# Putting the state and output products of each attention chunk in one place between feed-forward matmuls (Trainium2, one core)

## The chip, the cores and the metric

The kernel runs on one core of one Trainium2 chip. The metric is the device time of one execution in microseconds (us), the median over runs of the same kernel. The core has five engines with queues of their own: TensorE (PE), VectorE (DVE), ScalarE (ACT), GpSimd (POOL) and SyncE (SP, which issues DMAs). An engine executes its instructions in program order; where it needs another engine's result it waits on a semaphore.

## The reference

```python
# B=4, H=8, S=768, D=48: 3072 tokens of 384
for t in range(S):
    cur = einsum('bhd,bhe->bhde', u[None] * k[:, :, t], v[:, :, t])
    y[:, :, t] = einsum('bhd,bhde->bhe', r[:, :, t], state + cur)
    state = w[None, :, :, None] * state + einsum('bhd,bhe->bhde', k[:, :, t], v[:, :, t])
x = y.transpose(0, 2, 1, 3).reshape(B * S, H * D)
x = square(maximum(x @ w_in, 0)) @ w_out          # 384 -> 2048 -> 384
logits = x @ w_gate
noisy = logits + log1p(exp(x @ w_noise)) * noise  # 8 experts
top2, top2_w = softmax over the two largest of noisy
for e in range(8):
    out[tokens of e] += top2_w * (maximum(x @ w1[e], 0) @ w2[e])
```

Three stages in a row: a linear attention with a decaying state, a dense feed-forward layer with a squared ReLU, and a mixture of eight experts of which each token uses two. All inputs and outputs are float32.

## The kernel before, in words

**Tiles.** The 3072 tokens are cut into 24 attention chunks q of 128 tokens (six to a sequence; c = q % 6 is the place in its sequence) and into 6 feed-forward blocks j of 512 tokens, four chunks each. A list written out by hand (HEAD) does chunks 0 to 3. Block j from 0 to 4 then computes its own feed-forward layer and, in between, chunks 4(j+1) to 4(j+1)+3 for the next block. The experts follow behind block 5.

**A feed-forward block.** For f from 0 to 15 the program writes: mm1, nine matmuls of w_in (L540) into a bank ph; gsplit, in which ACT takes the ReLU and the square (L545, L551, L553) and VectorE the low half of the square (L555); the pieces of slot 2f; mm2 of f − 2, nine matmuls of w_out (L571; for some f six matmuls of L565); the pieces of slot 2f + 1. All of attention, of the router and of the conversion of weights inside a block is such a piece.

**What sets the order.** CHUNKS (lines 36 to 47) is a table of numbers. Row 0 is for block 0, row 1 for block 1, row 2 for blocks 2 to 4. For each of the four chunks of a block it holds nine numbers, the times of the nine pieces pre, p_tr r, p_tr k, pre2, p_kv, p_a, p_y 0, p_y 1 and p_x: the whole part of a number is the slot, and the fraction is the order inside the slot. All engines follow this order, since a piece writes its instructions for all of them when its turn comes.

**The pieces that matter.** p_a are the scores of a chunk: eight matmuls (L459) into two banks, which VectorE copies through a mask into am (L463). p_kv is the state product: sixteen small matmuls (L503) into a bank; VectorE adds the old state Z (L510) and POOL multiplies by the decay (L511), or VectorE multiplies alone where c is 0 (L513); where c is 5 nothing is done. p_y 0 is the output product with the state: twelve matmuls of rT and Z (L477), none where c is 0. p_y 1 is the output product with the chunk itself: sixteen matmuls of am with v or vx (L477) into the bank that p_y 0 took, and it issues the load of v of chunk q + 2. p_x reads that bank (ACT L522, VectorE L523). p_tr transposes r or k: on TensorE into a bank for chunks under 8 (L439; the result is scaled by VectorE at L444, or copied by ACT at L448), else on VectorE (L430) with a scaling on POOL (L432).

**Banks.** p_kv, p_a, p_y, p_tr and the router take their PSUM banks from three with the tag att. Each takes the one whose turn it is, and waits until its former user has been read out.

**Beside it.** In block 0 the weights are split into a high and a low half: conv_w1 (ACT L272), conv_w2 (VectorE L279, L280, L281 and then L291 or L288) and conv_w3 (ACT L301, POOL L302), on weights that SP's queue loads ahead. In the blocks behind it the router of the block before runs: products with the gate weights (L604), small VectorE steps (L631 to L667), ranking products (L705 to L709) and indirect DMAs on POOL that send tokens to their experts (L731, L732).

Of the kernel before, what the change touches and what calls it, by code (L numbers as in the profile page):

```python
# [34 lines left out]

CHUNKS = (((0.72, 2.09, 0.63, 0.83, 1.23, 3.2, 1.96, 5.12, 6.53),
# [11 lines left out]

WHOLE = (1, 3, 5)
SPLIT_AT = (1.5, 5.5, 9.5)  # L50
# [42 lines left out]
def body(ctx, tc, r, k, v, w, u, w_in, w_out, w_gate, w_noise, noise, w1, w2, out):  # L93
# [961 lines left out]
    for j in range(NB):  # L1055
# [6 lines left out]
        if j + 1 < NB:  # L1062
            for i, at_ in enumerate(CHUNKS[min(j, 2)]):
                q = (j + 1) * TPB + i
# [194 lines left out]
```

## Time and profile before

| | |
|---|---|
| median of three runs | 958.3 us (957.74 to 958.36) |
| profiled execution | 953.54 us |
| its span | 951.7 us |
| granted TensorE clock, mean | 0.998 |
| PE busy | 938.6 us, 99% |
| PE weight loads | 806.6 us, 85% |
| DVE busy | 539.5 us, 57% |
| ACT busy | 433.6 us, 46% |
| POOL busy | 349.7 us, 37% |
| block 0 starts (first L540) | 32.94 us |
| blocks 1 to 5 start | 118.64, 202.76, 285.95, 368.72, 452.36 us |
| first matmul of the experts (L853) | 525.04 us |

The span is that of the traced instructions in one execution; the execution's own time is 1.8 us more. Times in the trace are us from the span's start. Busy time is the sum of an engine's instructions without overlap; matmuls are pipelined, so the 0.39 us that a single one shows is not what it costs in a row of them. The chain of waits gives starts and durations that follow each other.

### The profile page before, as it was taken

The numbers are of one execution on the slowest core, as the hardware profiler recorded it, in microseconds if no ns is written. First come the engines' busy times: TensorE is split into PE (matmuls) and PEld (weight loads), VectorE is DVE, ScalarE is ACT, GpSimd is POOL, SyncE is SP. The second block draws the span as 40 slices with busy tenths as digits, with TensorE's granted clock in tenths as the row PEclk, the third lists the DMA queues.
The fourth block names the chain that finished last, engine by engine and source line by source line (L and its number), as shares of the span: only waits on it lengthen the run. The fifth ranks groups of instructions, "written<-read, shape, count | busy, mean of one in ns | idle before, by whom it ended". The sixth has DMA issues, their size and how long they took to land.

```text
span 951.7 us, 17753 instructions
## 1 busy us (share of the span) xinstructions
PE 938.6 (99%) x6845; PEld 806.6 (85%) x6845; DVE 539.5 (57%) x982; ACT 433.6 (46%) x792; POOL 349.7 (37%) x406
## 2 busy tenths in 40 slices
PE   8899999999999999999999999999999999999996
PEld 7677787788878878887888899999999898989986
DVE  8999757646845663583344563554545455456420
ACT  5666655344434444343555642443434444344321
POOL 6665353554563454455030353122121221212112
PEclk9999999999999999999999999999999999999999
DMA  7655379942432463341035368466545555555112
GB/s 177 164 162 163 102 193 297 247 111 63 104 94 56 126 162 107 102 115 70 1 101 122 88 143 180 102 131 146 120 96 117 119 119 120 103 100 114 23 21 38
DMA packets 193234, 112.33 MB, mean 118 GB/s; under 512 B 131777, under 2 KB 185698, under 8 KB 193122
## 3 DMA queue, kind: packets, MB, share of 16 engines
q1 hardware_dynamic: 181698, 91.03, 38.1%
q0 software_dynamic: 10624, 19.74, 11.3%
q8 instruction: 75, 1.23, 0.6%
q14 instruction: 37, 0.30, 0.1%
q10 hardware_dynamic: 800, 0.02, 0.0%
HBM read 74.64 MB, written 36.12 MB: 116 GB/s over the span
## 4 chain that ended last, share of the span: by engine, by line
PE 92%; DVE 4%; DMA 1%; issue 1%; ACT 0%; POOL 0%; POOLq 0%; ACTq 0%; DVEq 0%; SPq 0%
PE ph L540 20%; PE ph L853 20%; PE xo L571 19%; PE y L910 14%; PE y L941 5%; PE att L477 3%; PE ph L941 2%; PE att L459 2%; PE y L853 2%; PE att L604 2%; PE xo L565 1%; PE att L954 1%; PE att L503 1%; DVE am L463 1%; DVE t L280 1%
## 5 line engine op out<-in xcount | busy, mean ns | idle before, releaser
L921 POOL DMA_INDIRECT out<-yt,id x56 | 87.2, 1556 | 298.9 <-ACT yt L919 255.3
L555 DVE TENSOR_TENSOR gl<-g,gh 128x512 fp32r<-128x512 f32 x90 | 76.5, 851 | 137.5 <-ACT gh L553 137.2
L896 DVE SCALAR_TENSOR_TENSOR hl<-ph,hh 128x512 fp32r<-128x512 f32 (+1 forms) x112 | 67.0, 599 | 114.7 <-ACT hh L895 114.5
L545 ACT ACTIVATE rt<-ph 128x512 f32<-128x512 f32 x96 | 57.2, 595 | 152.5 <-PE ph L540 152.4
L540 PE MATMUL ph<-x1h,wih 128*128 128x512 f32 x288 | 119.3, 414 | 0.0
L853 PE MATMUL ph<-xh,w0h 128*128 128x512 f32 (+1 forms) x336 | 118.9, 354 | 0.0
L853 PE MATMUL ph<-xh,w0l 128*128 128x512 f32 (+3 forms) x336 | 116.3, 346 | 0.0
L853 PE MATMUL ph<-xl,w0h 128*128 128x512 f32 (+3 forms) x336 | 116.2, 346 | 0.0
L540 PE MATMUL ph<-x1h,wil 128*128 128x512 f32 x288 | 112.4, 390 | 0.0
L540 PE MATMUL ph<-x1l,wih 128*128 128x512 f32 x288 | 112.3, 391 | 0.0
L571 PE MATMUL xo<-gh,wol 128*128 128x512 f32 x270 | 105.9, 392 | 0.0
L895 ACT ACTIVATE hh<-ph 128x512 fp32r<-128x512 f32 (+1 forms) x112 | 58.7, 525 | 90.1 <-PE ph L853 89.8
L910 PE MATMUL y<-w1h,hh 128*128 128x384 f32 x256 | 85.7, 335 | 0.0
L910 PE MATMUL y<-w1l,hh 128*128 128x384 f32 x256 | 85.6, 335 | 0.0
L910 PE MATMUL y<-w1h,hl 128*128 128x384 f32 x256 | 85.6, 334 | 0.0
L732 POOL DMA_INDIRECT sent<-row,si x48 | 50.1, 1044 | 61.4 <-DVE gl L555 45.0
L571 PE MATMUL xo<-gh,woh 128*128 128x512 f32 x180 | 71.5, 397 | 0.0
L571 PE MATMUL xo<-gl,woh 128*128 128x512 f32 x180 | 70.1, 390 | 0.0
L853 PEld LDWEIGHTS ph<-xh,w0l 128*128 128x128 f32 x336 | 63.2, 188 | 7.8
L853 PEld LDWEIGHTS ph<-xl,w0h 128*128 128x128 f32 x336 | 63.3, 188 | 7.4 <-DVE xl L830 0.7
L853 PEld LDWEIGHTS ph<-xh,w0h 128*128 128x128 f32 x336 | 63.2, 188 | 6.6
L540 PEld LDWEIGHTS ph<-x1h,wih 128*128 128x128 f32 x288 | 54.0, 188 | 16.4 <-issue 3.7
(234 smaller groups left out, 2144.2 us busy)
## 6 DMA issues: line engine op xcount, KB each, us to landing
ws<-in_moe_w SPq DMA_DIRECT2D x128, 96.0 KB, 2.7
ws<-in_moe_w SPq DMA_DIRECT2D x32, 384.0 KB, 5.6
sent<-zero SPq DMA_DIRECT2D x8, 1375.5 KB
G<-sent SPq DMA_DIRECT2D x36, 192.0 KB, 3.3
stg<-in_moe_w_in SPq DMA_DIRECT2D x8, 768.0 KB
stg<-in_moe_w_out SPq DMA_DIRECT2D x8, 768.0 KB, 4.4
out<-zero SPq DMA_DIRECT2D x5, 960.0 KB, 6.0
lv<-in_v SPq DMA_DIRECT2D x24, 192.0 KB, 2.8
```

The costliest lines, as they stand in the source:

```text
L477: nc.tensor.matmul(pb[32 * n:32 * n + 32, d, :], x, y, skip_group_check=True, **kw)
L540: nc.tensor.matmul(ph, wt[qi][:, d, sl], xt[j][:, d, :], start=(n == 0), stop=(n == 3 * KD - 1))
L545: nc.scalar.activation(rt, ph, AF.Relu)
L555: nc.vector.tensor_tensor(gl, g, gh.bitcast(F32), op=OP.subtract)
L571: nc.tensor.matmul(XO[j][:, d, :], wt[qi][:, fo, sl], gt, start=(f == 0 and n == 0), stop=(f == NF - 1 and n == 2))
L732: st = nc.gpsimd.indirect_dma_start(out=sent, in_=s["row"][:, i, :], in_offset=None, out_offset=bass.IndirectOffsetOnAxis(ap=s["si"][:, i, ...
L853: nc.tensor.matmul(ph[:, c], wt[:, d, sl], xt[:, d, c], start=(m == 0), stop=(m == 3 * KD - 1))
L895: nc.scalar.activation(hh[:, :n], ph, AF.Relu)
L896: nc.vector.scalar_tensor_tensor(hl[:, :n], ph, 0.0, hh[:, :n].bitcast(F32), op0=OP.max, op1=OP.subtract)
L910: nc.tensor.matmul(py, ht[:, sl], wt[:, fo, :], start=(m == 0), stop=(m == 3 * NF2 - 1))
L921: st = nc.gpsimd.indirect_dma_start(out=out, in_=yt, in_offset=None, compute_op=OP.add, out_offset=bass.IndirectOffsetOnAxis(ap=IDX[e, un] ...
L941: nc.tensor.matmul(py[d][:, c], wt[:, fo, sl], ht[:, c], start=(m == 0), stop=(m == 3 * NF2 - 1))
```

## The change

Only numbers of CHUNKS change. For each of the four chunks of a block, p_kv, p_y 0 and p_y 1 now follow each other in one slot, mostly the slot that p_y 1 had, and p_a stands in a slot of its own. Of the second chunk of block 1 that slot is 18 (p_y 1 was at 22.37), of the third 27 (29.33), and the third's scores go from 27.97 to 24.8. For the third chunk of blocks 2 to 4 the transposition of r goes from 11.43 to 13.6. TensorE has 7268 rows in the program before and after.

```diff
-CHUNKS = (((0.72, 2.09, 0.63, 0.83, 1.23, 3.2, 1.96, 5.12, 6.53),
-           (3.99, 6.52, 7.82, 8.89, 12.58, 10.32, 14.31, 14.42, 14.572),
-           (8.79, 15.58, 15.74, 17.5, 17.09, 19.34, 20.21, 22.27, 28.57),
+CHUNKS = (((0.72, 2.09, 0.63, 0.83, 5.1, 3.2, 5.11, 5.12, 6.53),
+           (3.99, 6.52, 7.82, 8.89, 14.3, 10.32, 14.31, 14.42, 14.572),
+           (8.79, 15.58, 15.74, 17.5, 22.25, 19.34, 22.26, 22.27, 28.57),
            (18.59, 17.86, 20.56, 22.96, 28.05, 24.63, 28.23, 28.43, 29.69)),
-          ((0.1, 3.42, 3.92, 4.42, 4.47, 7.61, 9.16, 10.56, 12.58),
-           (7.94, 9.19, 9.32, 12.56, 21.33, 13.02, 18.64, 22.37, 25.05),
-           (15.73, 15.29, 22.28, 20.4, 22.63, 27.97, 26.35, 29.33, 29.51),
-           (22.4, 22.61, 24.26, 25.89, 28.2, 28.47, 30.02, 30.16, 31.3)),
-          ((0.79, 1.41, 3.65, 3.78, 7.94, 5.73, 11.24, 13.52, 15.46),
-           (5.03, 9.3, 9.79, 10.52, 13.32, 11.71, 13.34, 15.87, 17.6),
-           (14.31, 11.43, 15.7, 15.49, 23.64, 21.16, 19.91, 25, 25.46),
-           (18.6, 17.96, 19.29, 23.4, 25.47, 26.59, 26.24, 29.22, 29.82)))
+          ((0.1, 3.42, 3.92, 4.42, 10.54, 7.61, 10.55, 10.56, 12.58),
+           (7.94, 9.19, 9.32, 12.56, 18.62, 13.02, 18.63, 18.64, 20.6),
+           (15.73, 15.29, 22.28, 20.4, 27.7, 24.8, 27.71, 27.72, 29.51),
+           (22.4, 22.61, 24.26, 25.89, 30.14, 28.47, 30.15, 30.16, 31.3)),
+          ((0.79, 1.41, 3.65, 3.78, 13.5, 5.73, 13.51, 13.52, 15.46),
+           (5.03, 9.3, 9.79, 10.52, 15.85, 11.71, 15.86, 15.87, 17.6),
+           (14.31, 13.6, 15.7, 15.49, 25.01, 21.16, 25.02, 25.03, 25.46),
+           (18.6, 17.96, 19.29, 23.4, 29.2, 26.59, 29.21, 29.22, 29.82)))
```

Three places of the order, as the programs of before and of the change have it. The first is VectorE in block 0, before: the two additions to the state of chunk 4 (Z from the bank att) stand behind a reduction for chunk 5 and ahead of a weight conversion (t is the weight being converted).

```order
L414 TENSOR_REDUCE dg<-ra 128x8
L510 TENSOR_TENSOR Z_202<-att,Z_201 48x4x48 x2
L279 TENSOR_SCALAR t_722<-t_722 128x768
L280 TENSOR_SCALAR t_722<-t_722 128x768
L281 SCALAR_TENSOR_TENSOR t_722<-stg,t_722 128x768
```

VectorE, block 0, after, fourteen rows further on:

```order
L288 SCALAR_TENSOR_TENSOR woh_141<-stg,t_774 128x768
L279 TENSOR_SCALAR t_802<-t_802 128x768
L280 TENSOR_SCALAR t_802<-t_802 128x768
L281 SCALAR_TENSOR_TENSOR t_802<-stg,t_802 128x768
L291 SCALAR_TENSOR_TENSOR t_802<-stg,t_802 128x768
L510 TENSOR_TENSOR Z_202<-att,Z_201 48x4x48 x2
L444 TENSOR_TENSOR rT<-att,pow 112x512
```

The additions moved behind three conversions of weights, a low half of the square (L555) and the copies of chunk 4's scores (L463).

The second place is TensorE in block 0, before: the transposition of chunk 5's keys (kp) between mm2 and mm1, with the queues on which its first row waits.

```order
L571 MATMUL xo<-gl,woh_140 128x512
L571 MATMUL xo<-gh,wol_148 128x512
L439 MATMUL att<-ident,kp_98 112x128 [waits PE_49,Pool_49]
L439 MATMUL att<-ident,kp_98 112x128 x3
L540 MATMUL ph<-x1h,wih_126 128x512 [waits Activation_49]
```

The same place after:

```order
L571 MATMUL xo<-gl,woh_140 128x512
L571 MATMUL xo<-gh,wol_148 128x512
L439 MATMUL att<-ident,kp_98 112x128 [waits DVE_49,PE_49,Pool_49]
L439 MATMUL att<-ident,kp_98 112x128 x3
L540 MATMUL ph<-x1h,wih_126 128x512 [waits Activation_49]
```

The rows around the transposition are the same, and its first row has a wait on VectorE more.

The third place is TensorE in block 1, as a piece of the difference: the scores of chunk 10 (att from rT and kT) and, in the same slots, what came there from elsewhere.

```order
 L540 MATMUL ph<-x1l,wih_130 128x512
 L540 MATMUL ph<-x1h,wil_138 128x512
+L459 MATMUL att<-rT,kT 128x128 x8
 L571 MATMUL xo<-gh,wol_153 128x512
 L571 MATMUL xo<-gl,wol_153 128x512
-L571 MATMUL xo<-gh,wor_1812 128x512
+L571 MATMUL xo<-gh,wor_1778 128x512
```

The scores stand there three nines ahead of their place before.

## Rows read from the trace of the kernel before

**Rows 1.** The page's part 4: shares of the span in the chain that ended last.

```profile
PE 92%; DVE 4%; DMA 1%; issue 1%; ACT 0%; POOL 0%; POOLq 0%; ACTq 0%; DVEq 0%; SPq 0%
```

**Rows 2.** Chain in order of time, block 4: start us, us, engine, tile, line, matmul records.

```profile
388.01 0.48 PE att L503 x32
388.49 2.28 PE ph L540 x9
...
398.46 0.79 PE att L477 x24
399.25 1.09 PE att L459 x16
400.34 2.27 PE ph L540 x9
...
404.65 0.48 PE att L503 x32
405.13 1.53 PE att L477 x56
406.66 2.27 PE ph L540 x9
408.93 2.04 PE xo L571 x9
410.97 1.01 PE att L477 x32
411.98 2.26 PE ph L540 x9
...
430.93 0.48 PE att L503 x32
431.41 2.26 PE ph L540 x9
```

**Rows 3.** The same chain in block 1.

```profile
173.39 0.48 PE att L503 x32
...
174.03 2.15 PE ph L540 x9
176.19 1.01 PE att L477 x32
177.20 0.34 PE att L503 x32
177.54 2.26 PE xo L571 x9
```

**Rows 4.** Timeline of VectorE, blocks 0 and 4: start us, us, instruction.

```profile
40.22 0.73 DVE L510 TENSOR_TENSOR Z<-att,Z 48x192 f32<-48x192 f32 x2
...
47.28 1.41 DVE L279 TENSOR_SCALAR t<-t 128x768 f32<-128x768 f32 x1
...
53.28 0.55 DVE L279 TENSOR_SCALAR t<-t 128x768 f32<-128x768 f32 x1
...
55.45 0.96 DVE L291 SCALAR_TENSOR_TENSOR t<-stg,t 128x768 int32<-128x768 int32 x1
...
410.66 0.19 DVE L656 SCALAR_TENSOR_TENSOR nl<-oh,nl 128x32 f32<-128x32 f32 x1
```

**Rows 5.** Timeline of TensorE, block 0.

```profile
53.21 0.60 PE L439 MATMUL att<-ident,kp 128*112 128x128 f32 x4
...
70.49 0.86 PE L477 MATMUL att<-rT,Z 112*32 112x128 f32 x24
...
73.02 0.50 PE L571 MATMUL xo<-gh,woh 128*128 128x512 f32 x1
```

**Rows 6.** Timeline of POOL, blocks 0, 1 and 4 (in brackets idle before, and what ended it).

```profile
50.93 1.62 POOL L396 TENSOR_TENSOR ra<-ra,ub 128x384 f32<-128x384 f32 x1
...
181.30 1.29 POOL L432 TENSOR_TENSOR kT<-kT,pow 112x512 f32<-112x512 f32 x1
...
405.63 1.12 POOL L511 TENSOR_TENSOR Z<-Z,wmid 48x192 f32<-48x192 f32 x2 [2.33 <-DVE Z L510]
```

## The prediction

> **What bounds the kernel now.** I began with the page's chain of waits: 92% of the span is TensorE's and 1% is issue [rows 1]. Attention work therefore costs time in two ways: by the time that TensorE spends on its small matmuls, and wherever TensorE is made to wait for them. For the first I read the chain in blocks 4 and 1 [rows 2, 3]: it names TensorE alone there, and its pieces follow each other without a gap. What the reader is to see in it is a place, by which I mean the attention matmuls that stand between two nines (a nine is the group of nine feed-forward matmuls of L540 or L571), and that the nine behind a place is longer than one behind another nine. For the second I read the timelines of VectorE, TensorE and POOL around the steps that move [rows 4 to 6].
>
> **Prices of a place** (its own time and what the nine behind it has over 2.04, the plain one of 408.93) [rows 2]. State product alone: 0.48 + (2.26 − 2.04) = 0.70. Output product with am alone (part 1, 410.97): 1.01 + 0.22 = 1.23. Part 1 and a state product in one place: 1.01 + 0.34 + 0.22 = 1.57 [rows 3]. So a place that joins another saves 0.70 + 1.23 − 1.57 = 0.36. State and both output products: 0.48 + 1.53 + 0.23 = 2.24 [rows 2]; the product with the state (part 0) adds 2.24 − 1.57 = 0.67, and alone I price it at 0.67 + 0.36 = 1.03. Ahead of the scores part 0 takes 0.79 (398.46), and the scores behind it keep their 1.09 and the long nine when it goes: taking it away from there saves 0.79, which is 0.24 less than 1.03. A state product behind a router product takes 0.48, and the nine behind has 0.24 over 2.04 (388.49): 0.72, so nothing is shared there, and that counts as a place of its own. Beside the small ranking products of L705 to L709 I have no row that parts the two; sharing all would take the whole 0.36 from the saving, sharing nothing 0, and I take 0.18, since their nine of 2.15 lies between 2.04 and 2.26 [rows 3].
>
> **Joins, blocks 1 to 4.** Going through the order, places with a state or output product are 9, 8, 8 and 9 before and 4 in each block after: 18 joins. Five of the products that leave had stood ahead of scores (1, 2 and 2 in blocks 2, 3 and 4), three beside ranking (blocks 1, 2, 4). Block 1: 5 × 0.36 − 0.18 = 1.62. Block 2: 4 × 0.36 − 0.24 − 0.18 = 1.02. Block 3: 4 × 0.36 − 0.48 = 0.96. Block 4: 5 × 0.36 − 0.48 − 0.18 = 1.14. Together 4.74 us saved. No instruction is added or dropped.
>
> **Block 0: a new wait.** The three banks for attention are taken in turn. In the new order the transposition of chunk 5's keys (L439) gets the bank of chunk 4's state product, which VectorE frees with its two additions to Z (L510); the order now shows a wait on VectorE there. Those additions ran at 40.22 for 0.73; now they stand behind three weight conversions, the last step of which (L291) ends at 55.45 + 0.96 = 56.41 [rows 4], so they end near 57.14. TensorE reached the transposition at 53.21 [rows 5]: it waits 3.9. Ahead of it stands the output of chunk 4, which needs VectorE's copy of the scores (L463), so TensorE does not get there much earlier than before. If VectorE gets the 0.73 back that leaves at 40.22 and TensorE does not, the wait is 3.2; if conversions also start on earlier data, some 2.5, my lower end; upper end 4.2, with the place of chunk 4 longer by 0.34. VectorE itself loses nothing, and what is queued behind the additions (the scaling of rT, the low half of x) is used only after TensorE has gone on. Part is given back: chunk 5's output took 73.02 − 70.49 = 2.53 because the copy of its scores was late [rows 5], against 1.67 for both parts when nothing is late (2.24 less the 0.34 of the state product and 0.23 of the nine): 0.86. Chunk 6's join gives 0.36; chunk 4's is hidden, as TensorE waits for VectorE at that place anyway. Block 0: 3.9 − 0.86 − 0.36 = **+2.68**.
>
> **Block 1: a second wait.** The scores of chunk 10 move from 27.97 to 24.8 and need its keys, which POOL finishes (L432) at 181.30 + 1.29 = 182.59 [rows 6]. After the change the state product at 173.39 and the output place at 176.19 leave [rows 3], so TensorE gets there at 176.19 + 2 × 2.04 − 0.59 = 179.7, where 0.59 is 0.48 and the 0.11 that the nine at 174.03 has over 2.04. On POOL one multiplication of Z also leaves, half of 1.12 per chunk [rows 6] (0.5): keys at 182.1. The wait is **2.4**; 1.9 if POOL gains the whole 1.12, 3.1 if it follows none of the 0.72 that the two joins of chunk 8 give TensorE earlier. Block 1: 2.4 − 1.62 = +0.78.
>
> **Blocks 3 and 4: a short one.** The second chunk's part 0 now follows the first chunk's state closely. VectorE's router step L656 ends at 410.85 [rows 4], behind it (0.73 of another addition having gone ahead of it, 0.73 come) Z is added by 410.85 and multiplied on POOL by half of 1.12 [rows 6], at 411.41; part 0 would start at 410.97 + 0.34 = 411.31. With the crossing between engines I take 0.2 for each block (0 if VectorE is a step ahead, 0.5 if a step behind). In block 2 the first chunk starts a sequence and its state needs no POOL. Block 2 −1.02, block 3 −0.76, block 4 −0.94.
>
> **Moves that I cost at nothing.** The load of chunk 11's v (issued on SP behind part 1) moves ahead, past other loads; its use is over ten slots away. The third chunk's r transposition comes two slots later from block 2 on, on VectorE and POOL; its scores stand over seven slots behind. POOL's multiplications of Z pass conversions and sends; only the waits above have a matmul near behind.
>
> **Sum.** 2.68 + 0.78 − 1.02 − 0.76 − 0.94 = +0.74 on the profiled execution's 953.54, which lies 4.8 below the median of the runs; on the median 958.3 that is **959.0 us**. What a measurement of this kernel can tell from no change is about 0.2%, 1.9 us: that is no difference. Lower end of this case: −1.4 (block 0 at 2.5), −0.5, −0.4: 956.7. Upper: +0.3, +0.7, +0.6 and 0.5 of ranking: 961.1.
>
> **Rivals.** *A, the waits do not come* and only joins count: 4.74 + 0.36 saved, 953.2. For it: blocks 1 to 4 show no waits of TensorE before [rows 2, 3]. Against: the order shows the wait of block 0, and 56.41 against 53.21 is far apart. *B, slower:* the conversion ahead of Z runs at its slow price. Of the last two that stand there one takes from 47.28 to 53.28, 6.00, the other from there to 56.41, 3.13 [rows 4]; the slow one lies beside POOL's products that end at 50.93 + 1.62 = 52.55 [rows 6]. If POOL's products slide under the second conversion, Z ends 2.87 later: 959.0 + 2.9 = 961.9. It decides from 1.2 us of overlap on (960.2). Against it: POOL's trio is fed by loads and hardly moves. *C, joined places feed the state too slowly:* every chunk's part 0 waits for Z, ten places more at the 0.2 above, 961.0. In the trace for it is only the near miss of block 4; against it, the other chunks stand four slots or more apart. The Trainium skill (TensorEngine Tiling (Array Packing), PSUM Bottleneck) says that small tiles speed up TensorE and leave the emptying of PSUM as it was, which may become the limit; by that rule C is what happens, and in blocks 1 to 4 no row of before shows such a wait. *D, the change does not do what it says:* the order shows the products in one place; I give it nothing.
>
> **Chances.** Forecast 0.66, A 0.14, B 0.13, C 0.07. B and C lie above the bound; of the forecast case 0.10 lies beyond 960.2 and 0.03 below 956.4, and A is faster: faster 0.17, same 0.53, slower 0.30. The range 956.7 to 962.0 takes in B and C and leaves out A and some tail.
>
> **What will show it.** In the changed profile: places of about 2.24 with all three products in the chain; TensorE's L439 waiting some 3.9 for VectorE's Z (L510) near 53, and chunk 5's output without its wait; L459 waiting some 2.4 for POOL's kT (L432) near 182; L477 waiting 0.2 for Z in blocks 3 and 4. Block starts against before: +2.7 for block 1, then +3.5, +2.4, +1.7, and +0.7 from block 5 on. I am wrong if the first wait is under 2 or over 6, or if TensorE stops at a place that I have not named.

## The result, and the profile after

The changed kernel took **964.48 us** (median of 5 runs, 962.88 to 967.24), the kernel before beside it 957.74 (5 runs, 957.29 to 958.36): a ratio of 1.0073, 95% interval 1.006 to 1.0085. It is slower by 6.7 us, where 959.0 was forecast, in a range from 956.7 to 962.0. Its profiled execution took 965.15.

The lengths of the blocks (from one block's first L540 to the next one's; block 5 to the first L853) show where that went. The kernel "both stalls mended" is one of the experiments; the second profile of the change was taken in one of them.

| us | before | after | after, second profile | both stalls mended | forecast of the change |
|---|---|---|---|---|---|
| block 0 | 85.71 | 89.74 | 91.02 | 85.75 | +2.68 |
| block 1 | 84.11 | 89.29 | 86.59 | 82.47 | +0.78 |
| block 2 | 83.19 | 84.05 | 82.24 | 82.15 | −1.02 |
| block 3 | 82.77 | 84.25 | 81.80 | 81.80 | −0.76 |
| block 4 | 83.65 | 83.06 | 82.47 | 82.47 | −0.94 |
| block 5 | 72.68 | 73.55 | 72.97 | 72.63 | 0 |

The joins did what was forecast. The chain of the changed kernel in block 4 has the places of three products at 0.48 + 1.53 and 0.23 of the nine, 2.24, the price taken from [rows 2]:

```profile
414.50 0.48 PE att L503 x32
414.98 1.53 PE att L477 x56
416.51 2.27 PE ph L540 x9
```

What was not in the sum stands in the page's row of the granted clock (tenths of full speed, 40 slices), where before every digit is 9, and in the chain's shares, which answer to [rows 1]:

```profile
PEclk9989999899999999999999999999999999999999
...
PE 89%; DVE 5%; issue 2%; POOL 1%; ACT 1%; DMA 1%; SPq 1%; POOLq 0%; DVEq 0%; ACTq 0%
```

The longest waits of TensorE over the changed kernel's whole span (us in total, times, longest) name both forecast waits (the second and third line). The first line, "issue", is a kind of stop that no one had forecast:

```profile
PE att L477 <- issue: 2.8, 9, 0.3
PE att L459 <- POOL kT L432: 2.4, 1, 2.4
PE att L439 <- DVE Z L510: 2.3, 1, 2.3
PE att L477 <- DVE am L463: 1.9, 1, 1.9
```

The last line is chunk 4's place in block 0, where the prediction had TensorE wait for VectorE anyway. Before, the longest wait inside the blocks was 1.1 us, at chunk 4's scores in block 0, and it is gone after the change; no wait for a copy of scores was longer than 0.4:

```profile
PE att L459 <- DVE Z L510: 1.1, 1, 1.1
PE att L477 <- DVE am L463: 0.8, 3, 0.4
```

The chain through the first wait, in block 0 (the places of [rows 4] and [rows 5]):

```profile
54.80 0.96 DVE t L291
55.76 0.26 DVE Z L510
...
56.05 0.37 DVE Z L510
...
56.56 1.07 PE att L439 x4
57.63 3.22 PE ph L540 x9
```

The additions to Z stand behind the conversion, as the order said, and TensorE goes on when they are done. But the nine behind the wait takes 3.22 us and not some 2.1. The chain through the second wait, in block 1 (the places of [rows 3] and [rows 6]):

```profile
183.89 0.71 POOL sent L732
...
185.13 1.28 POOL kT L432
...
186.46 2.08 PE att L459 x16
188.54 4.14 PE xo L571 x9
...
197.04 0.48 PE att L503 x32
197.52 0.44 PE att L477 x16
197.96 0.31 issue
198.27 0.42 PE att L477 x5
198.69 0.32 issue
199.00 1.30 PE att L477 x35
```

The scores take 2.08 instead of 1.09 and the nine behind them 4.14 instead of 2.27. The stretches of the granted clock say why (us, then the busy time of TensorE's matmuls, its weight loads, VectorE, ScalarE and GpSimd, the granted clock, DMA share, GB/s):

```profile
186.28:193.10 6.82, 6.64 (x27) 5.45 (x28) 4.38 (x6) 0.00 (x0) 6.26 (x9) 0.50 0.82 185
56.57:59.98 3.41, 3.41 (x10) 2.85 (x11) 2.61 (x4) 1.47 (x3) 2.39 (x3) 0.50 1.03 299
46.33:49.74 3.41, 3.41 (x57) 2.93 (x50) 3.34 (x4) 1.66 (x4) 3.41 (x3) 0.50 0.67 223
```

TensorE ran at 0.50, the lower of its two levels (1.2 GHz instead of 2.4), for 13.7 us in three stretches, each beside the end of one of the three waits or just behind it (46.33 belongs to chunk 4's 1.9 us); before, the clock was at its full level from block 0 to the end of block 5. The last lines of block 1's chain show the third thing: pauses of 0.3 us inside the joined place, put down to "issue", with nothing that the trace shows to wait for. Five joined places of this profile were lengthened so, by 1.25, 1.90, 2.29, 0.15 and 0.59 us, 6.2 in all.

So two theories stood against the forecast. **Theory 1**: a stall of TensorE costs itself and then half clock; its rival: the stall alone counts. **Theory 2**: the pauses come where a long run of small matmuls meets a send of POOL (L732); its rival: they belong to the long run alone.

### The profile page after: what moved, and what is told of

The parts are those of the page before. It is cut to its first block, busy times and chain, and to the rows that moved or that the text cites. A ratio compares the mean times of both kernels' runs of the same rounds, so it can differ in the third digit from the quotient of the medians.

```text
span 963.4 us, 17747 instructions
## 1 busy us (share of the span) xinstructions
PE 941.7 (98%) x6845; PEld 811.0 (84%) x6845; DVE 544.5 (57%) x982; ACT 433.2 (45%) x792; POOL 348.0 (36%) x406
## 4 chain that ended last, share of the span: by engine, by line
PE 89%; DVE 5%; issue 2%; POOL 1%; ACT 1%; DMA 1%; SPq 1%; POOLq 0%; DVEq 0%; ACTq 0%
PE ph L853 19%; PE ph L540 18%; PE xo L571 17%; PE y L910 13%; PE y L941 5%; PE att L477 3%; PE ph L941 2%; PE att L459 2%; PE y L853 2%; PE att L604 2%; PE xo L565 2%; POOL sent L732 1%; PE att L954 1%; PE att L503 1%; DVE t L280 1%
## 5 line engine op out<-in xcount | busy, mean ns | idle before, releaser
L555 DVE TENSOR_TENSOR gl<-g,gh 128x512 fp32r<-128x512 f32 x90 | 77.8, 864 | 136.9 <-ACT gh L553 125.3
L540 PE MATMUL ph<-x1h,wih 128*128 128x512 f32 x288 | 119.8, 416 | 0.7 <-ACT rt L545 0.6
L853 PE MATMUL ph<-xh,w0h 128*128 128x512 f32 (+1 forms) x336 | 118.9, 354 | 0.0
L853 PE MATMUL ph<-xh,w0l 128*128 128x512 f32 (+3 forms) x336 | 116.3, 346 | 0.0
L853 PE MATMUL ph<-xl,w0h 128*128 128x512 f32 (+3 forms) x336 | 116.2, 346 | 0.0
L540 PE MATMUL ph<-x1h,wil 128*128 128x512 f32 x288 | 112.9, 392 | 0.0
L540 PE MATMUL ph<-x1l,wih 128*128 128x512 f32 x288 | 112.8, 393 | 0.0
L732 POOL DMA_INDIRECT sent<-row,si x48 | 50.1, 1044 | 60.1 <-DVE gl L555 49.5
L853 PEld LDWEIGHTS ph<-xh,w0l 128*128 128x128 f32 x336 | 63.2, 188 | 7.7
L853 PEld LDWEIGHTS ph<-xl,w0h 128*128 128x128 f32 x336 | 63.3, 188 | 7.5 <-DVE xl L830 0.9
L853 PEld LDWEIGHTS ph<-xh,w0h 128*128 128x128 f32 x336 | 63.3, 188 | 6.7
L540 PEld LDWEIGHTS ph<-x1h,wih 128*128 128x128 f32 x288 | 54.7, 190 | 16.7 <-issue 3.4
```

The lines of the kernel that those rows point to most:

```text
L540: nc.tensor.matmul(ph, wt[qi][:, d, sl], xt[j][:, d, :], start=(n == 0), stop=(n == 3 * KD - 1))
L555: nc.vector.tensor_tensor(gl, g, gh.bitcast(F32), op=OP.subtract)
L732: st = nc.gpsimd.indirect_dma_start(out=sent, in_=s["row"][:, i, :], in_offset=None, out_offset=bass.IndirectOffsetOnAxis(ap=s["si"][:, i, ...
L853: nc.tensor.matmul(ph[:, c], wt[:, d, sl], xt[:, d, c], start=(m == 0), stop=(m == 3 * KD - 1))
```

## The experiments

They were run in five jobs; kernels are compared with the kernel before of their own job. In jobs 1 and 5, as for the result, the kernel before took 956.5 to 957.7 us and every profile taken in those two jobs shows pauses; in jobs 2 to 4 none does, and it took 953.4 to 953.7.

**Job 1** (kernel before 956.54). First the kernel before, unchanged.

> The kernel before, unchanged, to see what its ordinary runs look like beside the one profiled execution, which took 953.54 us at a granted clock of 0.998 where the runs had 957 to 958. Theory 1 (TensorE's clock falls after a stall, and does so in some executions of the kernel before too): 957.7 us and a granted clock of 0.993 to 0.996, with a stretch at half clock in block 0. Rival (the difference lies in data traffic or the expert stage): 957.7 us with the clock at 0.998.

Measured: 956.85 us (ratio 1.0002, 0.9992 to 1.0011), and both guesses were wrong: the clock was full in blocks 0 to 5, and the time was in pauses. This is its chain at the place in block 3 where the state product follows part 1:

```profile
353.22 1.01 PE att L477 x32
354.23 0.40 PE att L503 x15
354.63 0.43 issue
355.06 0.31 PE att L503 x4
355.36 0.44 issue
```

and this the same place in the profile that the prediction read:

```profile
351.73 1.01 PE att L477 x32
352.74 0.34 PE att L503 x32
```

Two places of the kernel before paused, for 1.5 and 1.6 us: that is the 3 us by which this job's runs lay above its first profile. The forecast's frame had been an execution without pauses.

Next, one number of the change undone:

```diff
-CHUNKS = (((0.72, 2.09, 0.63, 0.83, 5.1, 3.2, 5.11, 5.12, 6.53),
+CHUNKS = (((0.72, 2.09, 0.63, 0.83, 1.23, 3.2, 5.11, 5.12, 6.53),
```

> The changed kernel with one number undone: the state product of chunk 4 back at 1.23. Theory 1 (that product's late additions to Z hold the bank, TensorE stalls 2.3 us in block 0 and then runs at half clock for stretches of 3.4 us): the stall and the low clock go, block 0 is as long as before (85.3 to 85.7 us against 89.7), total 964.5 - 4 = 960.5. Rival 1 (the stall alone counts, the clock is of no matter): 964.5 - 2.3 = 962.2. Rival 2 (block 0 is longer for another reason): 964.5.

Measured: 962.95 (1.0067, 1.005 to 1.0083); block 0 87.60. The wait of L439 and the low clock in block 0 are gone, so the mechanism is the one named, but only 2.1 of 4.0 us came back: with TensorE on time, the scores of chunk 7 now wait 1.4 us for chunk 6's state (VectorE L513), which the change had also put behind conversions. This wait was hidden as long as TensorE was late. The total by itself fits the first rival (962.2) better than the theory (960.5); it is the rows of block 0 that decide.

```diff
-           (15.73, 15.29, 22.28, 20.4, 27.7, 24.8, 27.71, 27.72, 29.51),
+           (15.73, 15.29, 21.6, 20.4, 27.7, 24.8, 27.71, 27.72, 29.51),
```

> The changed kernel with one number changed: the transposition of chunk 10's keys goes from 22.28 to 21.6, ahead of the first send on POOL, so that its scores find their keys ready. Theory 1 (stall of 2.4 and then 6.8 us at half clock, which cost 3.4): both go, 964.5 - 5.8 = 958.7. Rival (the stall alone): 964.5 - 2.4 = 962.1. A second rival (the send, now 1.3 later on POOL, holds up something else): over 962.

Measured: 961.25 (1.0042, 1.0025 to 1.0059). Block 1 fell from 89.29 to 85.03 with no wait and no low clock in it, although its two places beside sends paused for 2.5 us instead of 1.25: stall and clock were worth 4.26 + 1.25 = 5.5, as theory 1 had it and not 2.4. The total lies nearer to the rival's 962.1 than to the theory's 958.7, because the pauses of this profile add up to 8.9 us and not 6.2.

```diff
-           (14.31, 13.6, 15.7, 15.49, 25.01, 21.16, 25.02, 25.03, 25.46),
+           (14.31, 13.6, 15.7, 15.49, 22.81, 21.16, 22.82, 22.83, 25.46),
```

> The changed kernel with the joined place of the third chunk of blocks 2 to 4 moved from 25.0 to 22.8, ahead of the sends that POOL issues there. In the changed profile TensorE pauses for 0.3 us several times inside these three places, 4.8 us in all. Theory 2 (the pauses come where a long run of small matmuls meets the sends): the places take 2.24, 2.24 and 1.57 with what the nine behind has over 2.04, and the total is 964.5 - 4.8 = 959.7. Rival (the length of the run alone makes them): pauses at the new place as well, 964.5.

Measured: 966.43 (1.0103, 1.0086 to 1.012), and inconclusive: the edit brought a wait of its own. VectorE's copy of the scores (L463) stood behind router steps, and part 1 waited 1.8 us for it in block 2 and 3.6 in block 3. No pause was left in the three places, but only block 4's, with the wait near nothing, tells something: it was 0.4 us shorter.

**Job 2** (kernel before 953.58, no pauses in any kernel). The sends behind the third chunk's place:

```diff
-          25.32, 26.97, 30.88, 25.84, 25.99, 21.93, 31.39, 31.66),
-         (4.94, 7.82, 9.35, 9.61, 10.1, 13.34, 13.45, 13.47, 13.721, 14.31, 20.46, 19.12, 21.54,
-          24.75, 22.9, 28.29, 28.16, 23.33, 24.72, 21.55, 28.65),
+          25.32, 28.1, 30.88, 25.84, 28.2, 21.93, 31.39, 31.66),
+         (4.94, 7.82, 9.35, 9.61, 10.1, 13.34, 13.45, 13.47, 13.721, 14.31, 20.46, 19.12, 23.2,
+          25.9, 25.6, 28.29, 28.16, 25.7, 25.8, 25.5, 28.65),
```

> The changed kernel with the sends of the router moved behind the third chunk's joined place (blocks 1 to 4; the step that makes their indices goes from 21.54 to 23.2 in blocks 2 to 4). The five pauses in the changed profile add up to 1.25 + 1.90 + 2.29 + 0.15 + 0.59 = 6.2 us, and each stands where a send runs on POOL during the place. Theory 2 (a send beside a long run of small matmuls makes the pauses): none of them is left, and the kernel takes some 6 us less than the change: 0 to 2 us over the kernel before. Rival (the pauses belong to the long run at that point of the program, whatever POOL does): 6 to 7 us over the kernel before, as the change.

Measured: 956.65 (1.0033, 1.0023 to 1.0042). It tells nothing of theory 2, since the fourth chunks' places of blocks 2 to 4 did not pause either, with sends beside them.

Row 0 of CHUNKS as before the change:

> The changed kernel with row 0 of the table as before, so that block 0 is the kernel before's. Theory 1 (the stall and the half clock behind it in block 0 are this row's, and nothing of them is given back later): block 0 takes 85.7 us instead of 89.7, total 4.0 under the change, 2.7 over the kernel before. Rival (later blocks give part of the loss back, by work that is ready earlier): 1 to 2 under the change.

Measured: 952.79 (0.9992, 0.9983 to 1.0001); block 0 85.70. The whole loss of block 0 is the row's, and no later block had given any of it back. This block 0 holds something else that matters: behind a wait of 1.4 us for Z at chunk 4's scores the clock was at 0.50 for 3.41 us from 42.79, and the block is no longer for it. TensorE reached chunk 6's first transposition as early in the block as before (42.2 us after its start), because the waits for VectorE's copy of the scores between the two were gone or shorter (chunk 5's output took 1.98 instead of 2.53).

Row 0 as before, chunk 10's keys at 21.6 and the sends moved:

> Three mends at once: row 0 as before, chunk 10's keys ahead of the first send, the sends behind the third chunk's places. What is left of the change are the joins of blocks 1 to 4. Theory (the joins are worth the 4.7 us of the prediction, and stalls, clock and pauses were all that spoilt them): no stall, no half clock and no pause in blocks 0 to 4, blocks 1 to 4 of 82.5, 82.2, 81.8 and 82.5, total 949 to 950, 7 us under the kernel before, of which 2 to 3 are pauses that the kernel before has in its ordinary runs. Rival (a joined place costs more than the prices say): 953 to 957.

Measured: 948.55 (0.9945, 0.9933 to 0.9958); blocks 1 to 4 82.47, 82.15, 81.80, 82.47. The joins are worth what was forecast: 4.8 us in these blocks against 4.74.

Both stalls mended, the sends where the change has them:

> As the run with all three mends, but with the sends where the change has them: row 0 as before and chunk 10's keys ahead of the first send. Theory 1 and 2 together: 4.0 + 5.6 under the change, 3 us under the kernel before, with pauses of some 6 us left, so that the run with all three is 4 to 6 us faster. Rival (the pauses vary from run to run and cost little in ordinary runs): within 2 us of the run with all three mends.

Measured: 948.60 (0.9949, 0.9936 to 0.9962), no difference, as no place paused.

**Job 3** (953.65, no pauses). The change itself:

> The changed kernel, unchanged, because the kernel before took 956.5 us on the chip of the first four runs and 953.6 on that of the second four, and only the first showed pauses. If this chip's kernel before takes 956 or more: pauses beside the sends, and 6 to 8 us over the kernel before. If it takes 953 to 954: no pauses, and only the two stalls with their half clock are left, 4.0 + 5.6 - 4.7 = 4 to 5 us over it. Rival (the pauses are the change's own and come on any chip): 6 to 8 over it on either.

Measured: 957.38 (1.0037, 1.0022 to 1.0052), 3.7 us over the kernel before. Without pauses, the waits and the clock are all that is left. TensorE's waits:

```profile
PE att L439 <- DVE Z L510: 3.9, 1, 3.9
PE att L459 <- POOL kT L432: 2.4, 1, 2.4
```

and its chain in block 0:

```profile
56.14 0.37 DVE Z L510
...
56.65 1.07 PE att L439 x4
57.72 3.84 PE ph L540 x9
```

Both waits have exactly the length that was forecast, 3.9 and 2.4, and from the last 0.8 us of the first the clock was at 0.50 for 6.83 us, behind the second for 3.41. The wait of 1.9 us at chunk 4's place came here too, with no half clock behind it.

The sends moved, beside it:

> The run with the sends behind the third chunk's places, on the same chip as the run before this. On a chip with pauses: none at the third chunks' places, 4 to 6 us under the change beside it (theory 2); rival: pauses at the same places, no difference. On a chip without: within 1.5 us of the change.

Measured: 957.24 (1.0036, 1.0024 to 1.0049): no difference, as expected without pauses.

Both stalls mended:

> The mends of both stalls with the sends where the change has them. On a chip with pauses: pauses in three to five places beside sends, and a gain on the kernel before of 0 to 3 us; on a chip without: 5 us under the kernel before, as before. Rival: 5 us under it on a chip with pauses too, which would mean that the stalls have to do with the pauses.

Measured: 949.46 (0.9956, 0.994 to 0.9973).

The kernel before with chunk 4's line alone:

> The kernel before with the one line of chunk 4 changed (its state product at 5.1 and the output product with the state at 5.11). Theory 1: TensorE's transposition of chunk 5's keys waits 2.3 to 3.9 us for VectorE's additions to Z, the clock falls to half for 3.4 to 6.8 us behind it, block 0 takes 89.5 to 90.6 us, the total is 3.5 to 4.9 over the kernel before. Rival (the lateness is given back, as the prediction had it): 2.7 or less over it. Second rival (it needs the moves of chunks 5 and 6 too): no difference.

Measured: 957.79 (1.0045, 1.0028 to 1.0061); a wait of 3.9 us, half clock for 3.41 us behind it, block 0 90.08, all other blocks as before. One line of the table is enough for the loss of block 0.

**Job 4** (953.43, no pauses). This tells whether the half clock comes of TensorE's idleness. Row 0 is as before, and the stall of block 1 is filled with products that nobody reads:

```diff
         pbs = [bank(*tag), bank(*tag)]
+        for n in range(16 if q == 10 else 0):
+            nc.tensor.matmul(pbs[n % 2][:, :P], a["rT"][64 * (n % 2):64 * (n % 2) + D, n % HP, :],
+                             a["rT"][64 * (n % 2):64 * (n % 2) + D, n % HP, :], start=True, stop=True)
         for hp in range(HP):
```

> Row 0 as before, and the stall of block 1 filled: ahead of chunk 10's scores sixteen products of rT with itself go into the bank of the scores, which then overwrite them; nobody reads them. They take some 2.2 us in place of the 2.4 that TensorE waits. Theory (the half clock comes of TensorE's idleness and costs by itself): no stretch at half clock in block 1, block 1 takes 84.6 to 85.0 us, 1.7 to 3.4 less than in the same kernel unfilled. Rival (the clock is lowered whatever TensorE does, or costs nothing here): block 1 as in the unfilled kernel or longer, 86.5 to 88.1.

> The same kernel unfilled, beside it: a wait of 2.4 us for POOL's kT, then half clock for 3.4 or 6.8 us, block 1 of 86.4 or 88.1 us on a chip without pauses. Rival: as the filled one.

Measured: 951.01 filled (0.9975, 0.9965 to 0.9984) and 953.01 unfilled (0.9992, 0.9983 to 1.0002). The chain of the filled kernel (its lines are three further on), and its clock over the 3.41 us from 183.59:

```profile
183.88 1.16 PE att L462 x16
185.04 2.29 PE xo L574 x9
...
183.59:187.00 3.41, 3.12 (x25) 2.64 (x26) 2.60 (x3) 0.00 (x0) 3.33 (x4) 1.00 0.73 177
```

and the same of the unfilled one:

```profile
182.34 1.16 PE att L459 x16
183.50 3.84 PE xo L571 x9
...
183.59:187.00 3.41, 3.41 (x9) 2.63 (x10) 2.48 (x5) 0.00 (x0) 3.39 (x3) 0.50 0.83 177
```

In both the scores wait for the same keys of POOL; in the one TensorE has work for all but the last 0.5 us of that time, in the other none for 2.4. The nine behind takes 2.29 or 3.84, block 1 85.01 or 86.58. The half clock comes of the idleness, and it cost half of the time spent at it: 1.6 us of 3.41.

The two mended kernels again:

> All three mends. On a chip with pauses, theory 2 (sends make them): only the places that still have a send beside them pause (the second and fourth chunk's of blocks 1 and 2), and the gain on the kernel before is larger than the next run's. On a chip without pauses: 5 us under the kernel before.

> The mends of the two stalls with the sends as in the change. On a chip with pauses, theory 2: pauses at the third chunks' places of blocks 1, 2 and 4, 3 to 5 us slower than the run before this one; rival: the same pauses in both. On a chip without pauses: the same time in both, 5 us under the kernel before.

Measured: 949.34 (0.9957, 0.9941 to 0.9974) and 948.91 (0.9952, 0.9936 to 0.9969), without pauses no difference.

**Job 5** (956.73, with pauses, on the chip of job 3). The same two kernels:

> All three mends. If this chip's kernel before takes 956 or more (pauses), theory 2: no pause at the third chunks' places, pauses only where a send still stands beside a place, and a gain larger than the next run's by 2 us or more. If it takes 953 to 954: 5 us under it.

> The mends of the two stalls with the sends as in the change. On a chip with pauses, theory 2: pauses at the third chunks' places, 2 us or more over the run before this one; rival (the place in the program makes them): the same pauses in both and no difference. On a chip without: the same time in both, 5 us under the kernel before.

Measured: 961.59 with the sends moved (1.0054, 1.0036 to 1.0072) and 957.49 with the sends where the change has them (1.0008, 0.9998 to 1.0019). The time went the other way than either theory said, but the places tell why. The chain in block 2 with the sends of the change, first the third chunk's place, then the fourth's:

```profile
268.57 0.42 PE att L477 x12
268.99 0.17 issue
269.17 0.44 PE att L477 x6
...
282.29 0.48 PE att L503 x32
282.77 1.53 PE att L477 x56
```

and with the sends moved, in the same order:

```profile
268.91 0.48 PE att L503 x32
269.39 1.53 PE att L477 x56
...
281.11 0.21 PE att L477 x5
281.31 0.05 issue
281.37 0.42 PE att L477 x3
281.79 0.99 issue
```

POOL's sends ran at 267.14, 268.47 and 270.06 in the one, and at 278.20, 279.46, 280.72 and 282.33 in the other. The pauses went with them: from the third chunk's place (4.75 to 2.33 us, from the last matmul ahead to the first behind) to the fourth's (2.33 to 6.62). So theory 2 stands, its rival falls, and my edit was a bad one: it put a row of eight sends up against the fourth place of blocks 2 and 3, and half clock for 3.41 us followed the longer pauses in each (in block 3 of the other kernel too). Over the seven profiles that show pauses, 27 of the 28 lengthened places in blocks 1 to 4 (without the two of the early third chunk that waited for VectorE) had a send running in them or begun less than 1 us ahead. Of the 73 others 64 had none; 9 had one, but in five of these it began in the last 0.9 us of the place, and in four it had ended before the place's first record. Shorter places did not pause: in this job's two profiles all nine places of scores alone (16 records) beside sends took their plain time within 0.05 us, and in the kernel before of job 1 all nine places of up to 40 records beside sends did. In these profiles it took both, a long run and a send, and the joins make the long runs.

## Why the prediction was wrong

**Joins: right.** 18 joins at 0.36 less their corrections gave 4.74; blocks 1 to 4 of the mended kernel are 4.83 shorter than before (1.64, 1.04, 0.97, 1.18 against 1.62, 1.02, 0.96, 1.14).

**The two waits: right in place, cause and size**, 3.9 and 2.4 us where nothing else had slowed TensorE. The 3.9 is right in part because two shifts cancelled: without pauses TensorE came to that place 20.0 us into the block instead of 20.3, and Z was done at 23.8 instead of 24.2. In the profile of the result the first wait was 2.3, because TensorE got there later: the stretch of half clock from 46.33 stands ahead of it. The 0.86 given back at chunk 5's output came too: that place took 1.67 there.

**The step that failed** is the sum of each block with a wait: "Block 0: 3.9 − 0.86 − 0.36 = +2.68" and "Block 1: 2.4 − 1.62 = +0.78". They price a wait at its own length. With both came half clock for 3.41 or 6.83 us, of which half is lost, 1.7 or 3.4 (less where the stretch begins inside the wait). Block 1 of the second profile shows the missing term alone: 0.78 + 1.7 = 2.48, and it was 2.48 longer than before. Block 0 with it comes to 2.68 + 1.7 = 4.4 in the profile of the result and 2.68 + 3.0 = 5.7 in the second, and was 4.0 and 5.3 longer. With the term twice, the forecast of +0.74 would have been 3.4 to 6.8 us higher, +4.1 at its lower end, and 3.7 over the kernel before is what the change costs without pauses. In the profile that I read the clock was full through all blocks, and no wait in them was longer than 1.1 us; I took the full clock for granted when I added longer waits. The Trainium skill (TensorE: Matmul & The Clock Gate, HAM oscillation — how this bites in real kernels) says that a long enough wait in which TensorE idles throttles it again, so that the next work starts at half rate, and counts half of the throttled time as the loss. The filled stall agrees: 2.29 against 3.84 us for the same nine. Half clock that stands ahead of a later wait costs less or nothing: the first stretch in the profile of the result only shortened the wait behind it, from 3.9 to 2.3, and the one in block 0 of the kernel with row 0 as before left that block at 85.70.

**The frame** was the second failure. The sum was made in an execution without pauses and its result set on a median with some 3 us of them. That alone would have done no harm, had the change left the pauses as they were. It doubled them, 6.2 us against 3.1: long joined places now stood beside the sends at the third chunks, where the kernel before has two such places. 3.7 + 3.1 = 6.8 is near the 6.7 of the result; this is a rough sum, of a difference of medians without pauses and the pauses of two single profiles.

**The waits for Z in blocks 3 and 4** (0.2 each) did not come; blocks 3 and 4 are as short as the joins alone make them. Rival C falls with them: the mended kernel's joined places in blocks 1 to 4 show one such wait, of 0.2 us, in one of its five profiles without pauses. Rival B's slow conversion did not come either. Rival A is what the mended kernel does.

**What stays open.** What the state is in which places pause: one and the same chip showed none in job 3 and many in job 5, and the first profile of the kernel before has none, though the runs beside it took 957.3 to 958.4. Nor does any run show what TensorE lacks in a pause; in block 1 of the changed kernel's profile its weight loads stopped together with its matmuls, twice for 0.6 us. The Trainium skill (Runtime: NRT & Kernel Launch, Instruction fetch mechanics) holds instruction fetch for hidden behind the pace of dispatch. The traces have the packets of the instruction queues, and they do not show the pauses waiting for them: of the 62 gaps of over 0.3 us between matmuls in the lengthened places, 53 had no such packet under way, and one ended within 0.1 us of a packet's end. A table that keeps all long places clear of all sends was not tried.

The mended kernel, with row 0 as before and chunk 10's keys earlier, took 0.5% less than the kernel before in the three jobs without pauses, and the same (1.0008) in the one with them.

## What to carry to other kernels

Price a new wait of the matmul engine at its own length and then at half of the low-clock time that follows it, unless a later wait takes that up, above all in a kernel whose profile shows the clock full throughout; here a wait could be filled with idle products. When work is gathered into one place to save transitions, follow each of its results to the engine that reads them and each bank to whoever frees it: here one line of a table put two additions behind three conversions, and that cost about as much as all joins gained. Read more than one execution before a sum is set on a median.

## What the runs showed of the hardware that I had not expected

Places of 56 to 88 small matmul records paused in steps of 0.3 to 1.0 us while POOL issued indirect sends, and only in some jobs: the same place of the same kernel took 1.67 us in one execution and 3.28 in another. Heavy transfers without a send did not do it in the place where I looked. The window of the changed kernel around its joined place at 149 us, which took its plain time, has a DMA share of 1.06 and 359 GB/s in it:

```profile
149.00:152.00 3.00, 3.00 (x93) 2.36 (x93) 3.00 (x3) 0.00 (x0) 3.00 (x2) 1.00 1.06 359
```

How surely half clock came with a wait, over blocks 0 to 5 of all 20 profiles: with each of the 16 waits of 2.3 to 3.9 us (for 3.41 us in 12 of them and 6.83 in 4, which of the two differing between executions of the same kernel), with 4 of the 9 waits of 1.8 to 2.1 us and with 2 of the 13 of 1.1 to 1.8; the same wait of 1.9 us at chunk 4's place had it in one execution of the changed kernel and not in the other. Four more stretches stand behind pauses.
